# A norm split in two, gate derivatives from a table, stores on another queue, and 31 VectorE steps given to GpSimd

## The chip, the cores and the metric

The kernel runs on one core of a Trainium2 chip. Its time is the device time of one execution in microseconds (us), and the median of several runs is what counts. Engines are named as in the profile: PE (TensorE, matrix products; PEld is its weight load), DVE (VectorE), ACT (ScalarE), POOL (GpSimd), SP (SyncE, which here only issues DMAs).

## The reference

A sequence of 2048 positions with 512 channels is normalized; one branch is a short convolution of `k` times `v`, then a convolution over the whole sequence by FFT; the other is a gated MLP of width 1376. The kernel computes the output and the gradients of all nine inputs used.

```python
xn = _layernorm(A_q)
# branch s
k_shift = sum_t k_pad[:, t:t+S] * shift_k[:, ks-1-t]      # 4 taps
kv = k_shift * v
y  = irfft(rfft(kv, 2S) * rfft(ssm_k, 2S))[:S] + kv * ssm_D
s  = xn * y
# branch g
z  = (sigmoid(xn @ w_gate) * (xn @ w_up)) @ w_down
out = x + s * silu(z)
# returned: out, and the gradients for grad_out of A_q, A_k, A_v, A_shift_k, A_ssm_k, A_ssm_D, B_w_gate, B_w_up, B_w_down
```

## The kernel before

The sequence lies as 128 partitions by 16 rows (NJ). `p` counts 8 pairs of row tiles (256 positions), `cg` 4 groups of 128 channels, `q` two halves of an FFT block. Almost all of SBUF is one tile, `slab`, divided by hand, and PSUM is one tile, `psum`; so the profile names nearly everything `slab` and `psum`, and one line, L479, which calls every recorded operation.

The work falls into three stages that overlap.

- Front: `ln(p)` normalizes a pair of tiles (`bn_stats` and `bn_aggr` on DVE, the power −1/2 on GpSimd, the small product `nmr` on DVE, the scaling with its shift on DVE or ACT) and transposes the result; `gu_gen(p)` and `z_gen(p)` are the MLP; `strK`, `strV` and `strX` transform the long filter, build `kv` (four products over `lag`, 3 first, with sums between them) and go forward and back through the FFT. `step1`, `step2`, `inv2` and `inv1` are FFT steps as matrix products, each followed by an evacuation of PSUM (`evac`: on ACT or DVE, whichever queue holds it) and, for some, by a transpose on DVE.
- Middle: `zs_pre(p)` and `zs_gen(p)` form the gate silu(z), its derivative, `out_0` and `dz`; `dh_gen` and `x_gen` go back through the MLP. `zs_pre` runs two activations on ACT and three products and sums of 1024 columns on DVE for each pair.
- Back: `dW` makes the three weight gradients (`out_9`, `out_7`, `out_8`) with its operands loaded back transposed from DRAM (`hD`, `dgD`, `duD`), and stores each piece through one of three buffers `ot`; between its pieces `frontC` and `backC` carry the gradient of the convolution: products of 2048 columns with the kept spectra `KK` and `VV`, `inv2` and `inv1`, then `dks = dkv * v` and `dkv = dkv * ksh` for each `cg`, the four lags into `dk` (`out_2`), and `out_3` from `dkv`.

Nothing is scheduled while the kernel runs. All operations are first recorded with a number each; the table `ORDER` gives, for each of the five engines, the numbers in the order of its queue, and `BANKS` the PSUM bank of each tile. The `Rec.order` method checks that the queues can proceed and emits them. An engine works its queue strictly in order: an instruction that waits holds all behind it. DMAs stand in the queue of the engine that issues them, SP for nearly all.

Of the kernel before, what the change touches and what calls it, by code (L numbers as in the profile page):

```python
# [8 lines left out]
ACT = mybir.ActivationFunctionType  # L9
ALU = mybir.AluOpType  # L10
# [58 lines left out]
    """,  # L69
    "vector": """  # L70
# [1364 lines left out]
```

## Time and profile before

| | |
|---|---|
| runs | 469.19, 463.36, 464.43 us; median 464.43 |
| profiled execution, its own time | 466.05 us |
| its span, first to last instruction | 464.3 us |
| mean granted clock of TensorE | 0.987 |
| DMA | 117.13 MB in 188798 packets |

In the parts that follow, a group's line gives the engine, the operation, what is written from what (partitions x elements, type), the count, then busy us in all and the mean ns of one, then the idle time of the engine just before it and what ended it. A line of the timeline gives the start, the length, the engine, the operation and the count, and in brackets the wait ahead of it. A line of windows gives a stretch, its length, and the busy us of each engine with the number of instructions.

### The profile page before, as it was taken

What the parts mean: (1) busy time and instruction counts of PE and PEld (TensorE: products, weight loads), DVE (VectorE), ACT (ScalarE), POOL (GpSimd) and SP (SyncE); (2) the same over time, 40 slices, a digit from 0 to 9 for tenths busy, and PEclk for the clock granted to TensorE, in tenths of its full rate; (3) what the DMA queues carried; (4) which work ended last, traced back from release to release, by engine and by line L of the source; (5) the groups of instructions that cost most, each with busy time, mean ns of one, the idle gap of its engine ahead of it and who ended that gap; (6) DMA issues with size and microseconds to landing.
All of it is one profiled execution on the core that took longest, in us unless ns stands there. A gap on an engine that the chain in (4) does not pass through costs nothing.

```text
span 464.3 us, 11690 instructions
## 1 busy us (share of the span) xinstructions
PE 443.4 (95%) x4934; PEld 306.4 (66%) x4963; DVE 420.5 (91%) x634; ACT 287.8 (62%) x368; POOL 15.5 (3%) x31
## 2 busy tenths in 40 slices
PE   6998999999999999999999999999999799999994
PEld 3867785758667677556655664444467678877883
DVE  8999999999999899999999976679998799999991
ACT  7767898888667646565563433377744676855331
POOL 4200110010000000000000000000000000000000
PEclk8899899999999999999999999999999999999999
DMA  7999877869378799989689999799998999999997
GB/s 247 367 332 240 270 240 262 253 230 300 101 230 286 196 218 254 259 262 319 167 260 200 313 297 271 179 343 240 261 263 197 254 231 254 249 212 242 192 327 272
DMA packets 188798, 117.13 MB, mean 252 GB/s; under 512 B 107541, under 2 KB 175049, under 8 KB 188234
## 3 DMA queue, kind: packets, MB, share of 16 engines
q1 hardware_dynamic: 187546, 115.99, 92.3%
q8 instruction: 39, 0.64, 0.6%
q10 hardware_dynamic: 1200, 0.39, 0.4%
q14 instruction: 13, 0.11, 0.1%
HBM read 43.74 MB, written 46.70 MB: 195 GB/s over the span
## 4 chain that ended last, share of the span: by engine, by line
PE 60%; DVE 10%; DMA 6%; issue 2%; SPq 1%; ACT 1%; DVEq 0%; ACTq 0%
PE psum L479 60%; DVE slab L479 10%; DMA slab<-duD 3%; DMA slab<-KD 2%; SPq L479 1%; DMA slab<-VD 1%; ACT slab L479 1%; DMA out_dram<-slab 1%; DVEq L479 0%; ACTq L479 0%
## 5 line engine op out<-in xcount | busy, mean ns | idle before, releaser
L479 PE MATMUL psum<-slab 128*128 128x256 bf16 (+5 forms) x4934 | 443.4, 304 | 14.1 <-ACT slab L479 5.2
L479 PEld LDWEIGHTS <-slab 128*128 128x128 bf16 (+2 forms) x4963 | 306.4, 96 | 150.9 <-issue 39.0
L479 ACT CAST slab<-psum 128x1024 bf16<-128x1024 f32 (+4 forms) x233 | 202.4, 914 | 124.1 <-PE psum L479 71.3
L479 DVE TENSOR_TENSOR slab<-slab 128x1024 bf16<-128x1024 bf16 (+5 forms) x322 | 251.8, 821 | 21.5 <-ACT slab L479 13.3
L479 DVE STREAM_TRANSPOSE slab<-slab 128x1024 f32<-128x1024 f32 x48 | 76.2, 1591 | 2.4 <-ACT slab L479 1.6
L479 ACT ACTIVATE slab<-slab 128x512 bf16<-128x512 bf16 (+5 forms) x58 | 49.1, 880 | 26.3 <-DVE slab L479 24.5
L479 ACT ACTIVATE slab<-psum 128x512 bf16<-128x512 f32 (+1 forms) x56 | 32.3, 576 | 14.6 <-PE psum L479 13.3
L479 DVE CAST slab<-psum 128x1024 bf16<-128x1024 f32 (+2 forms) x32 | 34.2, 1073 | 6.4 <-PE psum L479 5.0
L479 DVE TENSOR_TENSOR slab<-psum,slab 128x512 bf16<-128x512 f32 (+2 forms) x52 | 31.2, 603 | 1.3 <-PE psum L479 1.1
L479 DVE SCALAR_TENSOR_TENSOR slab<-slab 128x2 f32<-128x2 f32 (+1 forms) x40 | 14.2, 366 | 1.5 <-POOL slab L479 1.2
L479 POOL MEMSET slab<- 128x128 bf16 (+3 forms) x10 | 5.2, 535 | 299.0 <-PE psum L479 153.0
L479 DVE TENSOR_SCALAR slab<-slab 128x512 bf16<-128x512 bf16 (+9 forms) x40 | 10.8, 285 | 0.2
L479 POOL TENSOR_TENSOR slab<-slab 128x2 f32<-128x2 f32 x8 | 8.3, 1039 | 74.5 <-DVE slab L479 74.5
L479 DVE BATCH_NORM_STATS2 slab<-slab 128x6 f32<-128x512 bf16 x16 | 10.5, 671 | 0.0
L479 ACT COPY slab<-psum 128x512 bf16<-128x512 bf16 (+1 forms) x9 | 6.7, 777 | 2.7 <-PE psum L479 2.6
L479 DVE SCALAR_TENSOR_TENSOR slab<-psum,slab 128x512 bf16<-128x512 f32 x8 | 5.5, 686 | 2.2 <-PE psum L479 2.1
L479 ACT ACT_TABLE_LOAD x4 | 5.1, 1283 | 2.3 <-issue 2.2
L479 DVE COPY slab<-psum 128x512 bf16<-128x512 bf16 (+1 forms) x9 | 4.8, 531 | 0.6 <-PE psum L479 0.6
L479 DVE MEMSET slab<- 32x192 uint32 (+3 forms) x10 | 1.4, 144 | 1.5 <-PE psum L479 1.1
L479 DVE BATCH_NORM_AGGREGATE slab<-slab 128x2 f32<-128x6 f32 x16 | 2.6, 165 | 0.0
L479 POOL IOTA slab<- 128x32 f32 (+3 forms) x8 | 2.0, 270 | 0.4 <-POOLq L1419 0.4
L479 ACT ACTIVATION_READ_ACCUMULATOR slab<-psum 128x1 f32 x8 | 1.6, 199 | 0.0
(10 smaller groups left out, 6.2 us busy)
## 6 DMA issues: line engine op xcount, KB each, us to landing
slab<-KD SPq DMA_DIRECT2D x16, 512.0 KB, 4.9
hD<-slab SPq DMA_DIRECT2D x8, 704.0 KB, 6.2
dgD<-slab SPq DMA_DIRECT2D x8, 704.0 KB, 7.0
duD<-slab SPq DMA_DIRECT2D x8, 704.0 KB, 4.8
slab<-in_A_k_dram SPq DMA_DIRECT2D x4, 1024.0 KB, 6.5
KD<-slab SPq DMA_DIRECT2D x8, 512.0 KB, 6.5
VD<-slab SPq DMA_DIRECT2D x8, 512.0 KB, 4.9
out_dram<-slab SPq DMA_DIRECT2D x16, 256.0 KB, 4.5
```

The lines of the kernel that those rows point to most:

```text
L479: getattr(getattr(self.nc, eng), meth)(*[place(v) for v in a], **{x: place(v) for x, v in k.items()})
```

## The change

1. The first norm (`p == 0`) is worked tile by tile: statistics and power of tile 0, then of tile 1, then the scalings. Its memset of the warm-up operand is on DVE, 13 warm-up matmuls stand for 10, and 5 more follow the transposes of the first two tiles. The tables for the FFT come after it in the recording, and the weights' first 256 columns before it.
2. The gate and its derivative come from ACT's tables `Silu` and `Derivative_silu`, two pairs at a time (`zs_batch`), for six of the eight pairs; the two pairs made inside `strG` keep `zs_pre`. ACT loads 11 tables for 4.
3. The weight gradients are evacuated on ACT alone and stored from ACT's queue, through 5 buffers `ot` for 3.
4. GpSimd gets the scaling of the norm for `p >= 2` (12), the product of lag 3 in `strV` (4), the sum `x + s` for `out_0` (8), `dkv * ksh` (4) and the product of lag 0 in `backC` but for the last group (3): 31 in all.
5. `ORDER` and `BANKS` are new throughout, and a sixth list, `moves`, gives the order of all DMAs over both issuing queues.

```diff
@@ ORDER
     "tensor": """
-        4+9 222 220 216 218 58+3 63+3 150+7 141+7 102+15 167+7 281 285+3 282+2 159+7 135+3 130+3 187+15 178 182+3
+        7+12 229 227 231 161+7 152+7 40 233 35+3 41+3 46+3 189+7 113+15 170+15 412+7 384+7 236+7 198+15 146+3 141+3
...
@@ Rec.order
-            for eng, q in queue.items():
+            for eng in self.ENGS:
+                q = queue[eng]
                 while at[eng] < len(q):
                     op = ops[q[at[eng]]]
+                    if moves and "dma" in op.alts[0][1] and moves[-1] != op.n:
+                        break
...
@@ ln
-        nc.vector.tensor_scalar_add(ve, sv[:, :, 7], LN_EPS)
-        nc.gpsimd.tensor_tensor(out=r, in0=ve, in1=neghalf.to_broadcast([P, 2]), op=ALU.pow)
-        nc.vector.scalar_tensor_tensor(nmr, sv[:, :, 6], -1.0, r, ALU.mult, ALU.mult)
-        for t in range(2):
-            u, m, b = x[:, t], r[:, t:t + 1], nmr[:, t:t + 1]
-            nc.add([("scalar", "activation", (u, u, ACT.Identity), dict(bias=b, scale=m))][p == 0:]
-                   + [("vector", "tensor_scalar", (u, u, m, b, ALU.mult, ALU.add), {})])
+        def stats(a, b):
...
+            nc.gpsimd.tensor_tensor(out=r[:, a:b], in0=ve[:, a:b], in1=neghalf.to_broadcast([P, b - a]), op=ALU.pow)
+        def norm(a, b):
+            nc.vector.scalar_tensor_tensor(nmr[:, a:b], sv[:, a:b, 6], -1.0, r[:, a:b], ALU.mult, ALU.mult)
+            for t in range(a, b):
+                u, m, c = x[:, t], r[:, t:t + 1], nmr[:, t:t + 1]
+                (nc.vector if p < 2 else nc.gpsimd).tensor_scalar(u, u, m, c, ALU.mult, ALU.add)
+        for a, b in ((0, 1), (1, 2)) if p == 0 else ((0, 2),):
+            stats(a, b)
+        for a, b in ((0, 1), (1, 2)) if p == 0 else ((0, 2),):
+            norm(a, b)
...
+                if p == 0:
+                    nc.vector.tensor_copy(dst, src)
+                    warm(x[:, t, 0:128], 3 * t + 1)
...
+    def zs_batch(ps_):
+        for p in ps_:
+            gate = T[p]["gate"] = wk["gate"].next()
+            nc.scalar.activation(gate, stA["zA"][:, 2 * p:2 * p + 2, :], ACT.Silu)
+        for p in ps_:
+            z = stA["zA"][:, 2 * p:2 * p + 2, :]
+            nc.scalar.activation(z, z, ACT.Derivative_silu)
...
-    nc.gpsimd.memset(warm_r.ap, 0.0)
+    nc.vector.memset(warm_r.ap, 0.0)
...
@@ strV
-                    nc.vector.tensor_tensor(acc, src, skl, ALU.mult)
+                    nc.gpsimd.tensor_tensor(out=acc, in0=src, in1=skl, op=ALU.mult)
@@ zs_gen
-        nc.vector.tensor_tensor(x, x, s, ALU.add)
+        nc.gpsimd.tensor_tensor(out=x, in0=x, in1=s, op=ALU.add)
@@ strZ
-            if "gate" not in T[p]:
-                zs_pre(p)
+            zs_next(n)
@@ dW
-                    nc.evac(ot[0:kf, :], acc[0:kf, :], 512)
-                    nc.sync.dma_start(out_9[f0 + b * 128:f0 + b * 128 + kf, :], ot[0:kf, :])
+                    nc.scalar.copy(ot[0:kf, :], acc[0:kf, :])
+                    nc.scalar.dma_start(out_9[f0 + b * 128:f0 + b * 128 + kf, :], ot[0:kf, :])
...
-                nc.evac(ot[:, :, 0:w], acc[:, :, 0:w], 2 * w)
+                nc.scalar.copy(ot[:, :, 0:w], acc[:, :, 0:w])
...
@@ backC
-            nc.vector.tensor_tensor(dkv, dkv, ksh, ALU.mult)
+            nc.gpsimd.tensor_tensor(out=dkv, in0=dkv, in1=ksh, op=ALU.mult)
...
-                    if lag == 0:
+                    if lag == 0 and cg < NG - 1:
+                        nc.gpsimd.tensor_tensor(out=dk, in0=src, in1=skl, op=ALU.mult)
+                    elif lag == 0:
                         nc.vector.tensor_tensor(dk, src, skl, ALU.mult)
```

What this does to the queues is seen at three places. GpSimd in the front, before: the 128x2 products are the powers of the norms, `1x768` the zeros ahead of a load of `k`.

```order
L479 TENSOR_TENSOR slab<-slab 128x2
L479 IOTA slab 128x32
L479 MEMSET slab 32x512
L479 TENSOR_TENSOR slab<-slab 128x2 x3
L479 MEMSET slab 1x768
L479 TENSOR_TENSOR slab<-slab 128x2 x2
L479 MEMSET slab 128x4x32
```

The same place after: 128x512 is the scaling of one tile, 128x2048 the product of lag 3.

```order
L492 TENSOR_TENSOR slab<-slab 128x2 x3
L492 TENSOR_SCALAR slab<-slab 128x512
L492 TENSOR_TENSOR slab<-slab 128x2
L492 TENSOR_SCALAR slab<-slab 128x512 x3
L492 TENSOR_TENSOR slab<-slab 128x2048
L492 TENSOR_SCALAR slab<-slab 128x512
L492 TENSOR_TENSOR slab<-slab 128x2
L492 TENSOR_SCALAR slab<-slab 128x512
L492 TENSOR_TENSOR slab<-slab 128x2
L492 TENSOR_TENSOR slab<-slab 128x2048
```

The powers, for which DVE waits, now stand behind scalings and products.

SP in the last third of the back, before: transposed loads (`duD`) and loads of kept tensors with the stores of `out_8` (128x2x256) between them.

```order
L479 DMA out_dram<-slab 128x2x256
L479 DMA slab<-VD_68 128x2048
L479 DMA slab<-slab 15x384
L479 DMA_TRANSPOSE slab<-duD_98 128x8x256 x2
L479 DMA out_dram<-slab 128x2x256 x2
L479 DMA slab<-kshD_60 128x2048
L479 DMA_TRANSPOSE slab<-duD_97 128x8x256
L479 DMA out_dram<-slab 128x2x256
L479 DMA_TRANSPOSE slab<-duD_98 128x8x256
```

ACT near its end, after: each store now follows evacuations (CAST from `psum`) on the same queue.

```order
L492 CAST slab<-psum 128x8x128
L492 DMA out_dram<-slab 128x2x256
L492 CAST slab<-psum 128x512
L492 DMA out_dram<-slab 128x2x256 x2
L492 CAST slab<-psum 128x512
L492 DMA out_dram<-slab 128x2x256
L492 CAST slab<-psum 128x128x8
```

SP keeps the loads and the stores of the other outputs; 35 stores moved over.

DVE near the end of the back, before: the first 128x16x128 sum belongs to the third channel group, the second is `dkv * ksh` of the last one, and 128x8x128 and 128x1024 are halves of the last group's lags.

```order
L479 TENSOR_TENSOR slab<-slab 128x2048
L479 TENSOR_REDUCE slab<-slab 128x4
L479 TENSOR_TENSOR slab<-slab 128x16x128
L479 TENSOR_TENSOR slab<-slab 128x1024
L479 TENSOR_TENSOR slab<-slab 128x8x128
L479 TENSOR_TENSOR slab<-slab 128x16x128
L479 TENSOR_TENSOR slab<-psum,slab 128x128
```

The same place after:

```order
L492 TENSOR_TENSOR slab<-slab 128x16x128
L492 TENSOR_TENSOR slab<-slab 128x2048 x2
L492 TENSOR_REDUCE slab<-slab 128x4
L492 MEMSET slab 32x192
L492 TENSOR_TENSOR slab<-slab 128x8x128
L492 TENSOR_TENSOR slab<-slab 128x16x128
L492 CAST slab<-psum 128x128x8
L492 COPY slab<-slab 128x1
```

The product with `ksh` is gone to GpSimd's queue, and an evacuation (128x128x8) that ACT had has come in its place.

More of the change, by code (lines that the diff above doesn't have):

```diff
@@ L33 @@
     "tensor": """
[35 rows of a table removed]
[29 rows of a table added]
     """,
     "vector": """
[26 rows of a table removed]
[23 rows of a table added]
     """,
     "scalar": """
[15 rows of a table removed]
[17 rows of a table added]
     """,
     "gpsimd": """
-        20 68 19 3 31+1 69 98 41 53 71+1 70 210 99 125 73 100 472 1628 883 906 1900 1297 2232 3538 4769
+        52 109 81 53 79+1 20 110 21 25 84 83 29 111 82 73 136 221 483 224 894 896 223 485 235 897 1911 486 1308 579
+        1914 1639 917 1913 1310+1 1078 1538 1642 1641 2278 2243 2419 2722 2855 2992 3123 3256 3383 3531 3921 4277 4762
+        4528 4681 5241 5398 5838
     """,
     "sync": """
[12 rows of a table removed]
[11 rows of a table added]
+    """,
+    "moves": """
[12 rows of a table added]
     """,
@@ L133 @@
 BANKS = (
-    "11312331001230100111001001100111000011100101101010101010110010110001110001010011011021013001101001100001110120"
-    "11000101100110011100011000110100110201301111010021112030101013323110130103201032101131010310122111230102312112"
-    "20012110031202212022032102122210023212013202301211212022210100203221102123221220123101210220300120131122203320"
-    "2202213202203023223032"
+    "02030110310012300101110310011302110011100101010101101201103010101110000011011031001010201031100101100111000001"
+    "21301110100110011002311001110010110010101100001011000211010101001130101010020011011013010003010311011001030011"
+    "20020210013210121202310220200201010232122122113021220102203202121030210221230022201221001021312002121303201220"
+    "213203212013101102002112"
 )
@@ L456, in order @@
                         owner[b] = v
-        seq, at = [], {e: 0 for e in queue}
+        seq, at, moves = [], {e: 0 for e in self.ENGS}, queue["moves"][::-1]
         while len(seq) < len(ops):
             had = len(seq)
-            for eng, q in queue.items():
+            for eng in self.ENGS:
+                q = queue[eng]
                 while at[eng] < len(q):
                     op = ops[q[at[eng]]]
+                    if moves and "dma" in op.alts[0][1] and moves[-1] != op.n:
+                        break
                     if not all(ops[d].done for d in op.deps) or any(w.left for v in op.tiles for w in before[id(v)]):
@@ L466, in order @@
                     op.done = True
+                    if moves and moves[-1] == op.n:
+                        moves.pop()
                     for v in op.tiles:
@@ L470, in order @@
             if len(seq) == had:
-                raise RuntimeError("the order is stuck at " + str({e: q[at[e]:at[e] + 1] for e, q in queue.items()}))
+                raise RuntimeError("the order is stuck at " + str({e: queue[e][at[e]:at[e] + 1] for e in self.ENGS}))
         return seq
@@ L685, in ln @@
         x, st = xnA[:, 2 * p:2 * p + 2, :], lnst.next()
-        for t in range(2):
-            nc.vector.bn_stats(st[:, 8 * t:8 * t + 6], x[:, t])
-        for t in range(2):
-            nc.vector.bn_aggr(st[:, 8 * t + 6:8 * t + 8], st[:, 8 * t:8 * t + 6])
         sv = st[:, 0:16].rearrange("p (t x) -> p t x", x=8)
@@ L692, in ln @@
         r = rstd_all[:, 2 * p:2 * p + 2]
-        nc.vector.tensor_scalar_add(ve, sv[:, :, 7], LN_EPS)
-        nc.gpsimd.tensor_tensor(out=r, in0=ve, in1=neghalf.to_broadcast([P, 2]), op=ALU.pow)
-        nc.vector.scalar_tensor_tensor(nmr, sv[:, :, 6], -1.0, r, ALU.mult, ALU.mult)
-        for t in range(2):
-            u, m, b = x[:, t], r[:, t:t + 1], nmr[:, t:t + 1]
-            nc.add([("scalar", "activation", (u, u, ACT.Identity), dict(bias=b, scale=m))][p == 0:]
-                   + [("vector", "tensor_scalar", (u, u, m, b, ALU.mult, ALU.add), {})])
+        def stats(a, b):
+            for t in range(a, b):
+                nc.vector.bn_stats(st[:, 8 * t:8 * t + 6], x[:, t])
+            for t in range(a, b):
+                nc.vector.bn_aggr(st[:, 8 * t + 6:8 * t + 8], st[:, 8 * t:8 * t + 6])
+            nc.vector.tensor_scalar_add(ve[:, a:b], sv[:, a:b, 7], LN_EPS)
+            nc.gpsimd.tensor_tensor(out=r[:, a:b], in0=ve[:, a:b], in1=neghalf.to_broadcast([P, b - a]), op=ALU.pow)
+        def norm(a, b):
+            nc.vector.scalar_tensor_tensor(nmr[:, a:b], sv[:, a:b, 6], -1.0, r[:, a:b], ALU.mult, ALU.mult)
+            for t in range(a, b):
+                u, m, c = x[:, t], r[:, t:t + 1], nmr[:, t:t + 1]
[4 more added lines that the diff above has]
+            norm(a, b)
         if p + 2 < NP:
@@ L707, in ln @@
                     nc.tensor.transpose(pt[:, db, :], x[:, t, db * 128:(db + 1) * 128], ident)
-                nc.evac(xnT[:, t].rearrange("p d k -> p (d k)"), pt[:].rearrange("p a k -> p (a k)"), 512)
+                dst, src = xnT[:, t].rearrange("p d k -> p (d k)"), pt[:].rearrange("p a k -> p (a k)")
+                if p == 0:
+                    nc.vector.tensor_copy(dst, src)
+                    warm(x[:, t, 0:128], 3 * t + 1)
+                else:
+                    nc.evac(dst, src, 512)
         else:
@@ L768, in zs_pre, with zs_next @@
         nc.vector.tensor_tensor(z, tm, sg, ALU.add)
+    def zs_batch(ps_):
[5 more added lines that the diff above has]
+            nc.scalar.activation(z, z, ACT.Derivative_silu)
+    def zs_next(n):
+        if "gate" not in T[ORD[n]]:
+            if n == 2:
+                wk["gate"].extend(wk["sg"])
+                wk["gate"].extend(wk["tm"])
+            zs_batch(ORD[n:n + 2])
     def ld_KT(cg, eng=None):
@@ L792, in ld_w, with warm @@
             e.dma_start(w[:, :, f0:f1], src[:, f0:f1].rearrange("(db p) f -> p db f", p=P))
+    def warm(w, n):
+        pw = ps("w", [512])
+        for _ in range(n):
+            nc.tensor.matmul(pw[:], w, warm_r.ap[:, 0:512], start=True, stop=True)
     f_ld(0)
+    ld_w(0, 256, nc.sync, nc.scalar)
     ld_KT(0)
     warm_r = Ring(ar, [640])
-    nc.gpsimd.memset(warm_r.ap, 0.0)
-    pw = ps("w", [512])
-    for _ in range(10):
-        nc.tensor.matmul(pw[:], warm_r.ap[:, 512:640], warm_r.ap[:, 0:512], start=True, stop=True)
-    ld_w(0, 256, nc.sync, nc.scalar)
+    nc.vector.memset(warm_r.ap, 0.0)
+    nc.vector.memset(neghalf, -0.5)
+    warm(warm_r.ap[:, 512:640], 13)
+    make_identity(nc, ident)
+    f_ln(0)
+    tabs = gen_fft_tables(nc, ar, negpi, halfpi, Cf)
     nc.scalar.dma_start(Dcol_b, A_ssm_D.rearrange("(cg p) -> p cg", p=P))
-    tabs = gen_fft_tables(nc, ar, negpi, halfpi, Cf)
-    make_identity(nc, ident)
+    f_ld(1)
     ld_w(256, 768, nc.sync, nc.sync)
     nc.sync.dma_start(skr, A_shift_k.rearrange("(o d) t -> o (d t)", o=1))
-    f_ld(1)
     ld_w(768, F, nc.sync, nc.sync)
@@ L811, in kernel_impl @@
     ld_v()
-    nc.vector.memset(neghalf, -0.5)
     nc.vector.memset(ones1, 1.0)
-    f_ln(0)
     gen_fft_consts(nc, ar, negpi, TT, I32, tabs)
@@ L1149, in strZ @@
             flags.add(("z", n))
-            if n + 1 < NP and "gate" not in T[ORD[n + 1]] and ("zf", ORD[n + 1]) in flags:
-                zs_pre(ORD[n + 1])
+            if n + 1 < NP and ("zf", ORD[n + 1]) in flags:
+                zs_next(n + 1)
     def strD():
@@ L1181, in kernel_impl @@
                        until=lambda: ("dh", 7) in flags)
-    for r in [WdT_r, x2_r, dzT_r, sig_r, h_r] + list(wk.values()):
+    for r in [WdT_r, x2_r, dzT_r, sig_r, h_r] + [wk[k] for k in ("s", "a", "gg", "gate")]:
         r.free()
@@ L1187, in kernel_impl @@
             (Ring, [NJ, GW], 1), (Ring, [512], 1), (Ring, [256], 1), (Ring, [GW], 1))
-    L_r, Xc_r, QV_r, QtV_r, ot_r = ar.rings((Ring, [NJ, 256], 3), (Ring, [2, 2048], 2), (WRing, 2048, 1), (WRing, 1024, 1), (Ring, [512], 3),
+    L_r, Xc_r, QV_r, QtV_r, ot_r = ar.rings((Ring, [NJ, 256], 3), (Ring, [2, 2048], 2), (WRing, 2048, 1), (WRing, 1024, 1), (Ring, [512], 5),
                                             freed=[b for r in dead for b in r.blks], then=late)
@@ L1229, in dW @@
                     ot = ot_r.next().rearrange("p (b f) -> p b f", b=2)
-                    nc.evac(ot[:, :, 0:w], acc[:, :, 0:w], 2 * w)
-                    nc.sync.dma_start(out[d2 * 256:(d2 + 1) * 256, f0:f0 + w].rearrange("(b p) f -> p b f", p=P), ot[:, :, 0:w])
+                    nc.scalar.copy(ot[:, :, 0:w], acc[:, :, 0:w])
+                    nc.scalar.dma_start(out[d2 * 256:(d2 + 1) * 256, f0:f0 + w].rearrange("(b p) f -> p b f", p=P), ot[:, :, 0:w])
             if n == 5:
```

178 rows, old and new, of the table ORDER are left out of this document.

## The prediction

> **What bounds the kernel now.** I read the page first, for the share of each engine.
>
> ```profile
> span 464.3 us, 11690 instructions
> PE 443.4 (95%) x4934; PEld 306.4 (66%) x4963; DVE 420.5 (91%) x634; ACT 287.8 (62%) x368; POOL 15.5 (3%) x31
> ...
> DVE  8999999999999899999999976679998799999991
> ...
> POOL 4200110010000000000000000000000000000000
> ...
> PE psum L479 60%; DVE slab L479 10%; DMA slab<-duD 3%; DMA slab<-KD 2%; SPq L479 1%; DMA slab<-VD 1%; ACT slab L479 1%; DMA out_dram<-slab 1%; DVEq L479 0%; ACTq L479 0%
> ```
>
> TensorE and VectorE are both nearly full, GpSimd is empty. TensorE holds 60% of the last chain, VectorE 10%. A share of the whole span hides stages, so the windows come next: front (12 to 156), middle (156 to 300), back (300 to 456).
>
> ```profile
> 0.00:12.00 12.00, 7.94 (x41) 4.53 (x42) 10.56 (x39) 9.10 (x10) 5.30 (x18) 0.84 0.80 251
> 12.00:36.00 24.00, 23.95 (x243) 18.48 (x243) 22.96 (x53) 17.14 (x24) 3.01 (x7) 0.94 0.99 344
> 36.00:48.00 12.00, 10.53 (x127) 8.54 (x125) 11.96 (x22) 10.33 (x13) 0.84 (x1) 0.90 1.18 265
> 48.00:60.00 12.00, 11.95 (x113) 8.80 (x113) 11.38 (x18) 10.36 (x14) 1.93 (x3) 0.95 0.72 208
> 60.00:84.00 24.00, 22.42 (x284) 15.45 (x283) 23.42 (x27) 20.58 (x26) 1.19 (x1) 1.00 0.84 270
> 84.00:156.00 72.00, 71.49 (x915) 50.43 (x920) 71.16 (x76) 54.01 (x72) 1.80 (x2) 1.00 0.71 231
> 156.00:300.00 144.00, 143.26 (x937) 89.09 (x950) 127.77 (x259) 73.28 (x103) 0.73 (x1) 1.00 0.97 250
> 300.00:360.00 60.00, 58.74 (x782) 33.59 (x788) 53.90 (x54) 38.10 (x45) 0.00 (x0) 1.00 1.00 253
> 360.00:372.00 12.00, 9.53 (x142) 7.65 (x141) 8.86 (x8) 7.65 (x9) 0.00 (x0) 1.00 1.10 259
> 372.00:456.00 84.00, 82.06 (x1338) 68.51 (x1337) 78.14 (x84) 46.05 (x56) 0.73 (x1) 1.00 1.04 247
> 456.00:465.00 9.00, 1.50 (x33) 1.36 (x32) 0.36 (x1) 1.21 (x3) 0.00 (x0) 0.84 0.58 219
> ```
>
> After the length stand the busy times of PE, PEld, DVE, ACT and POOL, then the clock granted to TensorE. In the front PE is busy 140.3 of 144 us (3.7 idle) and DVE 140.9 (3.1 idle): both bind. In the middle PE is full (0.7 idle) and DVE has 16.2 us to spare. In the back PE has 5.7 us idle of 156, DVE 140.9 busy and 15.1 idle. So a faster VectorE can win at most the 9.4 us of PE idle in front and back, plus something at the two ends; a slower VectorE costs soon in the front and later in the back.
>
> **The change, part by part.** First what is taken from DVE, and the one thing that can be said of GpSimd's prices.
>
> ```profile
> L479 DVE TENSOR_TENSOR slab<-slab 128x2048 bf16<-128x2048 bf16 x109 | 129.9, 1211 | 7.1 <-DMA slab<-KD 3.1 <-ACT slab L479 2.1 <-DMA slab<-VD 1.0
> L479 DVE TENSOR_TENSOR slab<-slab 128x1024 bf16<-128x1024 bf16 x150 | 97.3, 684 | 4.9 <-ACT slab L479 3.2 <-DVE slab L479 0.8
> ...
> L479 DVE CAST slab<-psum 128x1024 bf16<-128x1024 f32 x25 | 30.1, 1209 | 1.1 <-PE psum L479 0.8
> ...
> L479 POOL TENSOR_TENSOR slab<-slab 128x2 f32<-128x2 f32 x8 | 8.3, 1039 | 74.5 <-DVE slab L479 74.5
> ...
> L479 DVE TENSOR_SCALAR slab<-slab 128x512 bf16<-128x512 bf16 x13 | 5.6, 440 | 0.0
> ...
> L479 ACT ACT_TABLE_LOAD x4 | 5.1, 1283 | 2.3 <-issue 2.2
> ...
> L479 POOL MEMSET slab<- 1x768 bf16 x4 | 2.9, 727 | 248.0 <-DVE slab L479 146.0 <-PE psum L479 102.0
> ...
> L479 POOL MEMSET slab<- 128x640 bf16 x1 | 0.6, 631 | 0.0
> ```
>
> DVE loses 11 products of 2048 columns (4 in the convolution of the front, 7 in the back), 13.3 us; 26 steps of 1024 columns (18 of the gate derivatives, 8 sums of out_0), 17.8 us; 9 scalings, 4.0 us. The new order gives it 8 more evacuations of 1024 columns, 9.7 us. Net it is some 25 us lighter.
>
> GpSimd takes 11 products, 8 sums and 12 scalings (3 of these from ScalarE). No trace shows it on such tiles. Its memsets of 640 and 768 columns differ by 96 ns, 0.75 ns a column. A product reads two operands and writes one: between one and three times that rate, plus up to the 0.69 us of its smallest product (quoted next), gives 1.5 to 5.3 us for 2048 columns. I take 3.5, between the ends, since no row is nearer to either; 1.8 for 1024 and 1 for a scaling: about 65 us in all, which fits into an idle engine.
>
> The price lies elsewhere: do the two engines run side by side? The timeline of DVE and POOL, at two places:
>
> ```profile
> 46.99 1.22 DVE L479 TENSOR_TENSOR slab<-slab 128x2048 bf16<-128x2048 bf16 x1
> 47.16 1.59 POOL L479 TENSOR_TENSOR slab<-slab 128x2 f32<-128x2 f32 x1 [12.88 <-DVE slab L479]
> ...
> 48.78 0.16 DVE L479 SCALAR_TENSOR_TENSOR slab<-slab 128x2 f32<-128x2 f32 x1 [0.58 <-POOL slab L479]
> ```
> ```profile
> 12.54 0.69 POOL L479 TENSOR_TENSOR slab<-slab 128x2 f32<-128x2 f32 x1 [0.24 <-DVE slab L479]
> ...
> 13.34 0.74 DVE L479 TENSOR_SCALAR slab<-slab 128x512 bf16<-128x512 bf16 x1
> 13.41 0.52 POOL L479 MEMSET slab<- 32x512 bf16 x1
> ```
>
> The same two-column power takes 0.69 us at 12.54 and 1.59 at 47.16, where it starts inside a DVE product and ends 0.54 us after it (48.75 against 48.21): GpSimd was held until the product was over. The other way round, a DVE scaling beside a GpSimd memset takes 0.74 us against a mean of 0.44 and ends 0.15 us after the memset: VectorE was held. So I count a DVE product that comes up while a GpSimd product runs as held to its end. The Trainium skill has this as a rule (SBUF — State Buffer, "Who interferes with whom"): a DVE instruction with two SBUF inputs contends with a GpSimd instruction that reads SBUF, and whoever starts first keeps the shared ports for its whole instruction. The rows agree, except that none shows a DVE product held. GPSIMD Engine Reference, section 3.1, measures 4497 ns for a 2048-column fp32 tensor_tensor on GpSimd; with that price in place of my 3.5 us the sum below would come to about 476.
>
> How much of each is held follows from how often DVE meets such a product; its groups in the front, then in the back:
>
> ```profile
> L479 DVE TENSOR_TENSOR slab<-slab 128x2048 bf16<-128x2048 bf16 x48 | 57.5, 1209 | 0.5 <-ACT slab L479 0.2
> ```
> ```profile
> L479 DVE TENSOR_TENSOR slab<-slab 128x2048 bf16<-128x2048 bf16 x61 | 72.3, 1213 | 6.7 <-DMA slab<-KD 3.1 <-ACT slab L479 1.9 <-DMA slab<-VD 1.0
> ...
> L479 DVE TENSOR_TENSOR slab<-slab 128x1024 bf16<-128x1024 bf16 x14 | 9.4, 686 | 0.9 <-DVE slab L479 0.8
> ...
> L479 DVE TENSOR_TENSOR slab<-slab 128x512 bf16<-128x512 bf16 x5 | 2.0, 400 | 0.0
> ```
>
> *Start.* Today PE waits 1.83 us for the first norm; below, the row, and the weight load that now stands ahead of the second input tile on ScalarE's queue.
>
> ```profile
> 8.46 1.04 PE L479 MATMUL psum<-slab 128*128 128x128 bf16 x8 [1.83 <-DVE slab L479]
> ```
> ```profile
> 1.64 0.53 ACTq L479 DMA_DIRECT2D slab<-in_B_w_up_dram  x1
> ```
>
> The norm of one tile no longer waits for the other; the second tile's issue moves back by 0.53 us behind the weights. Taken −1 us; bounds −2.5 (wait and some cold clock gone) and +0.5 (the late tile decides).
>
> *Front.* Other DVE work between two products averages (140.9 − 57.5) / 48 = 1.7 us, so a 3.5 us product holds DVE for 1.8: four of them, 7.2. Twelve scalings are shorter than that gap: 0.3 each, 3.6. Less 4.8 + 4.0 freed, that is +2 on DVE, which has 3.1 idle. Taken +1. Also the power now stands in GpSimd's queue behind products; behind it DVE's scaling waits (0.58 us above), and with that all evacuations queued there: up to 4.5 us once, in the upper bound. Bounds −4 (not held, PE's idle gone) to +8.
>
> *Middle.* 17.8 us off DVE count nothing: PE is full. ScalarE takes 7 table loads, 9.0 us, into 70.7 us of its own idle time; if an evacuation is due just then, PE waits up to 1.3 us each. The 8 sums write out_0 only; the buffer they free is due a stage later. Taken 0; bounds −0.5 to +4.
>
> *Back.* Two-input products are 83.7 of 140.9 us, in 80 pieces: 0.7 us between two, so a 3.5 us product holds DVE for 2.8. Seven: 19.6; less 8.5 freed, plus about 3 of the added evacuations: +14 on DVE against 15.1 idle, of which the KD and VD loads keep part. I let 9 be absorbed: +5. Bounds −5 (not held) to +15.
>
> *Stores.* Weight-gradient stores go from SyncE's queue to ScalarE's, with 5 output buffers for 3.
>
> ```profile
> ACT slab L479 <- DMA out_dram<-slab: 20.7, 7, 5.1
> ```
> ```profile
> 448.89 2.91 ACT L479 CAST slab<-psum 128x1024 bf16<-128x1024 f32 x4 [5.11 <-DMA out_dram<-slab]
> ```
> ```profile
> 450.44 1.74 PE L479 MATMUL psum<-slab 128*128 128x96 bf16 x34 [0.46 <-ACT slab L479]
> ```
>
> ScalarE stands 20.7 us for buffers, but PE feels 0.46 us of it here, and loads behind SyncE's stores some more. 35 issues at about 0.5 us fit ScalarE's 64 us of idle time in the back. What is late next is the last matmul and its store, which stay. Taken −2; bounds 0 to −4.
>
> Sum: 464.3 − 1 + 1 + 0 + 5 − 2 = 467.3. The profiled execution took 466.05, 1.75 outside its span, and the median shown is 464.43, 1.6 lower; both together add 0.1. **467 us.**
>
> **Rivals.**
>
> *The lock decides (slower).* Place: the back. If a product on GpSimd takes over 4 us, DVE's 15 us of idle time are used up and each further microsecond goes to PE. At 4.4 us, halfway from my value to the upper end: back 7 × 3.7 + 3 − 8.5 − 9 = +11, front 4 × 2.7 + 3.6 − 8.8 − 3 = +3: 464.3 − 1 + 3 + 11 − 2 = 475. At 5.3, the end: back +18, front +6, 485. For it: both directions of holding are in the trace. Against it: the holding pow reads two columns only, and a product may let go between pieces. Chance 0.30, 474 to 488.
>
> *GpSimd runs free (faster).* A product on it doesn't hold DVE. Then the 9.4 us of PE idle in front and back go, or most of it: 464.3 − 1.5 − 3 − 4 − 2 = 454. For it: the cover of 25 us on DVE is real. Against it: the 1.59 us row. Chance 0.18, 450 to 460.
>
> *Nothing moves.* PE is its own bound, DVE's idle absorbs every hold, and the stores' waits were hidden: 463. Chance 0.10.
>
> **How the numbers follow.** My forecast, 460 to 474 around 467, has 0.42. A measurement of this kernel tells about 2% from no change: 455.1 and 473.7. Faster: most of the free case, 0.15. Slower: nearly all of the lock case and the upper end of the forecast, 0.33. Same: 0.52. The range runs from 454 to 482; about a tenth lies beyond either end. The forecast's own is 460 to 474.
>
> **What would show it.** Right: GpSimd products of 3 to 4 us; DVE products of 2048 columns with a tail of 2 us and more over 1.21 at those places; DVE's busy time in the back not below today's 140.9; ScalarE's wait for out_dram gone; PE's first transposes earlier by a microsecond. Wrong: products on DVE still at 1.21 us while GpSimd works (then the free case), GpSimd products over 4.4 us (then the lock case), or a power behind a product for which DVE waits more than 3 us at several places.

## The result, and the profile after

The changed kernel takes 489.28 us (median of 4 runs, 488.47 to 490.78) against 464.83 for the kernel before in the same session: ratio 1.0502, 95% interval 1.0452 to 1.0553. The ratio is taken over the fast runs of both kernels, so it differs a little from the quotient of the medians, 1.0526. The change is slower by 5%, outside the range forecast. The profiled execution took 488.47 us, its span 486.7.

The page of the changed kernel first: span, busy times, and the rows of DVE and POOL in 40 slices.

```profile
span 486.7 us, 11716 instructions
PE 448.9 (92%) x4938; PEld 307.4 (63%) x4971; DVE 434.1 (89%) x595; ACT 289.0 (59%) x368; POOL 93.8 (19%) x62
...
DVE  7889899999998788898988897899996998989993
...
POOL 4227342133000022120111010000024430025020
...
PE psum L492 10%; DVE slab L492 5%; DMA out_dram<-slab 2%; ACTq L492 0%; ACT slab L492 0%; DVEq L492 0%
```

GpSimd works 78.3 us more, as the diff says. But VectorE, with 39 instructions fewer, is busy 13.6 us *longer*. The chain at the end of the page covers only the last fifth of this span, so its 10% for PE can't be set against the 60% of before. The groups say which of DVE's instructions grew (count, then busy us in all and mean ns of one):

```profile
L492 DVE TENSOR_TENSOR slab<-slab 128x2048 bf16<-128x2048 bf16 x98 | 135.0, 1396 | 3.0 <-DMA slab<-KD 1.1 <-ACT slab L492 0.7 <-DMA slab<-in_A_k_dram 0.2
L492 DVE TENSOR_TENSOR slab<-slab 128x1024 bf16<-128x1024 bf16 x124 | 89.5, 752 | 7.5 <-ACT slab L492 5.1 <-DMA slab<-hD 0.9 <-PE psum L492 0.5
...
L492 DVE CAST slab<-psum 128x1024 bf16<-128x1024 f32 x33 | 40.0, 1215 | 5.7 <-PE psum L492 5.0 <-ACT slab L492 0.4
...
L492 POOL TENSOR_TENSOR slab<-slab 128x2048 bf16<-128x2048 bf16 x11 | 49.4, 4499 | 169.6 <-DMA slab<-kshD 66.9 <-DVE slab L492 58.3 <-ACT slab L492 18.2
L492 POOL TENSOR_TENSOR slab<-slab 128x1024 bf16<-128x1024 bf16 x8 | 18.8, 2346 | 149.9 <-DVE slab L492 114.1 <-DMA slab<-in_A_q_dram 29.7 <-PE psum L492 6.1
L492 POOL TENSOR_SCALAR slab<-slab 128x512 bf16<-128x512 bf16 x12 | 13.2, 1104 | 1.3 <-DVE slab L492 1.3
```

The mean of a DVE product with both operands in `slab` went from 1211 to 1396 ns at 2048 columns, from 684 to 752 at 1024; an evacuation from PSUM stayed (1209, now 1215). So DVE as a whole did not become slower. The timeline shows where the added time sits, at three places (start, length, engine, operation):

```profile
105.72 6.18 DVE L492 TENSOR_TENSOR slab<-slab 128x2048 bf16<-128x2048 bf16 x2
...
105.71 5.11 POOL L492 TENSOR_TENSOR slab<-slab 128x2048 bf16<-128x2048 bf16 x1 [18.19 <-ACT slab L492]
...
111.96 0.41 PE L492 MATMUL psum<-slab 32*32 32x512 bf16 x8 [3.49 <-DVE slab L492]
...
362.22 1.97 DVE L492 STREAM_TRANSPOSE slab<-slab 128x1024 f32<-128x1024 f32 x1
364.22 1.23 DVE L492 CAST slab<-psum 128x1024 bf16<-128x1024 f32 x1
...
361.87 4.06 POOL L492 TENSOR_TENSOR slab<-slab 128x2048 bf16<-128x2048 bf16 x1 [66.89 <-DMA slab<-kshD]
...
385.24 10.05 DVE L492 TENSOR_TENSOR slab<-slab 128x2048 bf16<-128x2048 bf16 x2
...
385.02 8.05 POOL L492 TENSOR_TENSOR slab<-slab 128x2048 bf16<-128x2048 bf16 x2
...
395.34 0.62 PE L492 MATMUL psum<-slab 32*32 32x512 bf16 x8 [5.29 <-DVE slab L492]
```

At 105.7 two DVE products, 2.4 us of work, take 6.18, and PE stands 3.49 us for what follows them. At 361.9 a GpSimd product runs beside a DVE transpose and a DVE evacuation, and neither is lengthened. At 385.0 GpSimd has two products back to back, and two DVE products end only at 395.29, 2.2 us after the second; PE has then stood 5.29 us. Summed over the trace (each DVE instruction's length over the usual one of its shape, where it overlaps a GpSimd instruction; stream transposes left out, which have two usual lengths, 1.2 and 2.0 us), DVE was held 35.6 us: 10.7 beside the 4 products of the front, 10.1 beside the 8 sums, 14.4 beside the 7 products of the back, 0.6 beside the 12 scalings. How that reaches TensorE is in the waits (us in total, times, longest), of the kernel before first:

```profile
PE psum L479 <- DVE slab L479: 3.6, 3, 1.8
```
```profile
PE psum L492 <- DVE slab L492: 23.2, 20, 5.3
...
ACT slab L492 <- DMA out_dram<-slab: 6.9, 3, 3.1
```

PE waited 3.6 us for DVE before, now 23.2. ScalarE's wait for store buffers fell from 20.7 to 6.9, as the change intended. The windows place it (length; busy PE, PEld, DVE, ACT, POOL; granted clock):

```profile
84.00:156.00 72.00, 63.79 (x803) 44.69 (x814) 68.23 (x60) 52.88 (x66) 11.11 (x4) 0.95 0.59 188
156.00:300.00 144.00, 137.54 (x1009) 86.82 (x1022) 128.63 (x229) 84.38 (x113) 19.65 (x10) 1.00 0.94 250
...
372.00:456.00 84.00, 75.02 (x1191) 60.53 (x1190) 79.27 (x63) 42.74 (x53) 20.30 (x6) 0.96 1.02 226
```

PE lost 7.7 us of busy time in the front's window (71.49 before), 5.7 in the middle, which had been full (143.26), and 7.0 in the back (82.06). In either trace some 30 matmul records are missing (29 and 33, against the weight loads), so each of these is good to about a microsecond.

Waiting is not all of it. The clock of the first and the last of these windows was 1.00 before and is 0.95 and 0.96 now. The drops lie at three long waits of PE, of 2.79, 3.49 and 5.29 us, which end at 89.3, 112.0 and 395.3:

```profile
89.50:92.90 3.40, 3.40 (x27) 2.90 (x25) 3.40 (x5) 1.93 (x2) 0.00 (x0) 0.50 0.24 86
113.40:116.80 3.40, 3.40 (x32) 1.88 (x30) 3.27 (x5) 2.49 (x4) 0.00 (x0) 0.50 0.61 182
393.30:400.10 6.80, 4.25 (x39) 2.38 (x39) 6.71 (x7) 2.84 (x3) 0.00 (x0) 0.50 1.12 287
```

What that is worth is seen below, where two kernels with the same matmuls are compared. That the waits cause the drops is not shown: in a later run (the fills below) the clock also fell to 0.50 from 125.5 on, with no wait of PE over 1.3 us before it in the whole front.

### The profile page after: what moved, and what is told of

Same layout as the page of the kernel before. It is cut to its first block, busy times and chain, and to the rows that moved or that the text cites. A ratio compares the mean times of both kernels' runs of the same rounds, so it can differ in the third digit from the quotient of the medians.

```text
span 486.7 us, 11716 instructions
## 1 busy us (share of the span) xinstructions
PE 448.9 (92%) x4938; PEld 307.4 (63%) x4971; DVE 434.1 (89%) x595; ACT 289.0 (59%) x368; POOL 93.8 (19%) x62
## 5 line engine op out<-in xcount | busy, mean ns | idle before, releaser
L492 PE MATMUL psum<-slab 128*128 128x256 bf16 (+5 forms) x4938 | 448.9, 306 | 31.9 <-DVE slab L492 23.2
L492 ACT CAST slab<-psum 128x1024 bf16<-128x1024 f32 (+4 forms) x229 | 197.1, 902 | 161.5 <-PE psum L492 104.3
L492 DVE TENSOR_TENSOR slab<-slab 128x1024 bf16<-128x1024 bf16 (+4 forms) x285 | 255.8, 932 | 14.8 <-ACT slab L492 7.1
L492 POOL TENSOR_TENSOR slab<-slab 128x2048 bf16<-128x2048 bf16 (+3 forms) x28 | 74.3, 2657 | 341.0 <-DVE slab L492 193.9
L492 ACT ACTIVATE slab<-slab 128x512 bf16<-128x512 bf16 (+5 forms) x55 | 47.0, 886 | 16.9 <-DVE slab L492 16.7
L492 DVE CAST slab<-psum 128x1024 bf16<-128x1024 f32 (+2 forms) x36 | 42.0, 1170 | 8.7 <-PE psum L492 8.0
L492 DVE SCALAR_TENSOR_TENSOR slab<-slab 128x2 f32<-128x2 f32 (+2 forms) x41 | 17.9, 440 | 3.7 <-ACT slab L492 3.4
L492 POOL TENSOR_SCALAR slab<-slab 128x512 bf16<-128x512 bf16 x12 | 13.2, 1104 | 1.3 <-DVE slab L492 1.3
L492 DVE BATCH_NORM_STATS2 slab<-slab 128x6 f32<-128x512 bf16 x16 | 10.7, 679 | 0.0
L492 POOL MEMSET slab<- 128x128 bf16 (+2 forms) x9 | 4.2, 471 | 28.6 <-DVE slab L492 17.9
L492 DVE TENSOR_SCALAR slab<-slab 128x2 f32<-128x2 f32 (+9 forms) x32 | 6.6, 232 | 0.1
```

Of the source, the lines that this page charges most:

```text
L492: getattr(getattr(self.nc, eng), meth)(*[place(v) for v in a], **{x: place(v) for x, v in k.items()})
```

## The experiments

**Theory.** A DVE instruction with two operands in SBUF is held while a GpSimd instruction reads SBUF, and these holds are the 5%. **Rivals.** The new order, the split norm or the stores cost it; or GpSimd's results come late and their consumers wait.

**All 31 steps back.** Everything else of the change stays: first norm, gate tables, stores, order of the other engines.

```diff
-                    nc.gpsimd.tensor_tensor(out=acc, in0=src, in1=skl, op=ALU.mult)
+                    nc.vector.tensor_tensor(out=acc, in0=src, in1=skl, op=ALU.mult)
...
-        nc.gpsimd.tensor_tensor(out=x, in0=x, in1=s, op=ALU.add)
+        nc.vector.tensor_tensor(out=x, in0=x, in1=s, op=ALU.add)
...
-            nc.gpsimd.tensor_tensor(out=dkv, in0=dkv, in1=ksh, op=ALU.mult)
+            nc.vector.tensor_tensor(out=dkv, in0=dkv, in1=ksh, op=ALU.mult)
...
-                        nc.gpsimd.tensor_tensor(out=dk, in0=src, in1=skl, op=ALU.mult)
+                        nc.vector.tensor_tensor(out=dk, in0=src, in1=skl, op=ALU.mult)
```

(and the same for the scalings in `ln`; in `ORDER` their numbers go from the list `gpsimd` into `vector`).

> The changed kernel with all 31 steps back on VectorE, each put into VectorE's queue where GpSimd had begun it in the trace of the changed kernel; everything else (first norm, gate tables, stores, order of the other steps) stays. Lock theory (a product on VectorE is held while GpSimd reads SBUF; 35.6 us of held time in the trace): the held time goes and about 25 us of work return to VectorE, so PE's extra idle time of 23 us goes almost wholly: 462, between 457 and 468. Rival (the new order, the gate tables or the stores cost the time): still above 480.

Measured: 469.62 us (10 runs), ratio 1.0021, interval 0.9983 to 1.0059. Of its page and its waits:

```profile
PE 448.2 (96%) x4971; PEld 306.5 (65%) x4971; DVE 419.3 (89%) x626; ACT 288.7 (62%) x368; POOL 14.7 (3%) x31
```
```profile
PE psum L492 <- DVE slab L492: 9.8, 15, 1.3
```

DVE does 31 steps more than in the changed kernel and is busy 14.8 us *less*; the longest wait of PE for DVE falls from 5.3 to 1.3 us. So the 31 steps carry the loss, and what is left of the change is worth nothing that can be measured here. It is not the gain expected, 462 us with 468 as the upper end: that part of the expectation missed.

**One kind of step at a time.** The same edit for the 11 products alone, the 8 sums alone and the 12 scalings alone.

> Only the 11 products of 2048 columns go back to VectorE; 8 sums and 12 scalings stay on GpSimd. Lock theory: 25.0 us of the 35.6 us held go, and with them the gaps of PE at 86, 108 and 390 us (2.95, 3.66 and 5.64 us); left are the stalls of the middle, some 6 us: 470, between 465 and 475. Rival (order): above 480.

> Only the 8 sums of 1024 columns go back to VectorE. Lock theory: 10.1 us of held time go, and the PE stalls of about 0.75 to 1.3 us beside each sum in the middle: 489 less 5 to 7, so 483. Prediction's own term for the middle (0, PE is full there): 489, no change.

> Only the 12 scalings of the norms go back to VectorE. Lock theory: they held VectorE for 0.6 us in all, so nothing comes back, and 12 x 0.4 us of work goes to VectorE in the stage where it is nearly full: 489 to 494. If GpSimd's scalings cost by the powers queued behind them: below 486.

Measured: products back 473.69 us, ratio 1.0132 (1.0094 to 1.0170); sums back 484.79, 1.0365 (1.0334 to 1.0397); scalings back 491.50, 1.0492 (1.0434 to 1.0551). Against the changed kernel's 1.0502, from the session before, the products are worth 3.7 points, the sums 1.4, and the scalings 0.1, which is inside the intervals of about 0.6 either way: no cost of a scaling on GpSimd is shown, and no gain. PE's busy time and its waits for DVE, of the kernel with the products back, and then of that with the sums back:

```profile
PE 448.2 (95%) x4971; PEld 306.3 (65%) x4971; DVE 422.9 (90%) x606; ACT 288.3 (61%) x368; POOL 47.7 (10%) x51
...
PE psum L492 <- DVE slab L492: 11.0, 15, 1.3
```
```profile
PE 452.2 (94%) x4971; PEld 308.6 (64%) x4971; DVE 428.4 (89%) x603; ACT 288.8 (60%) x368; POOL 75.6 (16%) x54
...
PE psum L492 <- DVE slab L492: 21.0, 13, 5.8
```

The products make the long waits, of up to 5 us and more. The sums make a few short ones in the middle: with them on GpSimd PE stands idle 4.5 us there (between the marks used further below), in waits of up to 1.2 us; with all 31 steps back it is 0.6. And where the products stay on GpSimd, the same 4971 matmuls take 4.0 us longer (452.2 for 448.2), at a mean granted clock of 0.977 for 0.991: that much of their cost is not waiting.

**Is it the reading?** GpSimd is kept as busy, but with fills in place of products and sums.

```diff
+def BESIDE(nc, out, in0, in1, op):
+    n = out.shape[1]
+    nc.gpsimd.tensor_tensor(out=out[:, 0:1, 0:1], in0=in0[:, 0:1, 0:1], in1=in1[:, 0:1, 0:1], op=op)
+    nc.gpsimd.memset(out, 0.0)
+    nc.gpsimd.memset(out[:, n // 4:n], 0.0)
...
+                if op.n in GIVEN:
+                    BESIDE(self.nc, **k)
+                    continue
```

> The changed kernel, with each of the 11 products and 8 sums that GpSimd got replaced on GpSimd by a tensor_tensor of one element (it keeps the wait for both inputs) and two fills of the same output region, of 2048 and 1536 columns (1024 and 512 for a sum). So GpSimd is occupied about as long (some 3.5 us for a product by the 0.95 us per 1000 columns of the 768-column fill), but reads almost no SBUF while it is; the products and sums are not computed (the outputs are zeros there). Theory (DVE instructions with two SBUF inputs are held while a GpSimd instruction reads SBUF): no held DVE products are left beside these, the time falls to that of the kernel with all 31 steps back, 469.6, or up to 4 us below it, since DVE does not do those steps: 466 (462 to 472). Rival 1 (the results come late from a slow engine, and their consumers wait): as long as the changed kernel, 485 to 490. Rival 2 (writes of GpSimd hold DVE too): 480 to 490, with held products beside the fills.

Measured: 464.25 us (10 runs), ratio 0.9933 (0.9896 to 0.9971). The groups of DVE and POOL:

```profile
L496 DVE TENSOR_TENSOR slab<-slab 128x2048 bf16<-128x2048 bf16 x98 | 117.5, 1217 | 3.2 <-DMA slab<-KD 1.3 <-ACT slab L496 0.8
L496 DVE TENSOR_TENSOR slab<-slab 128x1024 bf16<-128x1024 bf16 x124 | 81.2, 685 | 10.0 <-ACT slab L496 7.0 <-DMA slab<-hD 1.5 <-PE psum L496 0.5
...
L505 POOL MEMSET slab<- 128x2048 bf16 x11 | 19.9, 1807 | 3.8 <-ACT slab L496 3.2
L506 POOL MEMSET slab<- 128x1536 bf16 x11 | 15.2, 1378 | 0.6
```

And its timeline at the front's last product:

```profile
100.44 2.32 DVE L496 TENSOR_TENSOR slab<-slab 128x2048 bf16<-128x2048 bf16 x2
...
100.00 1.80 POOL L505 MEMSET slab<- 128x2048 bf16 x1
101.86 1.38 POOL L506 MEMSET slab<- 128x1536 bf16 x1
```

The same 98 and 124 DVE products are back at 1217 and 685 ns; two of them take 2.32 us beside the fills where they took 6.18 beside a product. GpSimd is busy 3.52 us for each product's place (0.34 for the one element, 1.81, 1.38), a little less than a product's 4.06, so lateness is cut too, by about half a microsecond; but a fill that held DVE's products would have shown in the means. Nor did the zeros that the fills leave raise the granted clock (0.985 in the profiled execution, 0.991 with all 31 back). What holds DVE's two-operand products is the reading. The Trainium skill says just this (SBUF — State Buffer, "Who interferes with whom"): two SBUF inputs on DVE contend with a GpSimd instruction that reads SBUF, not with one that only writes. Both halves agree with these runs. But a fill is not free for all of DVE: once, at 34.45, a TENSOR_SCALAR of 128x128, which has one tensor operand, took 1.92 us beside a fill, and in the other kernels it takes 0.21 to 0.23.

This kernel leaves out work, so it is no candidate; it shows about the most that these 31 steps could bring in this order if GpSimd did not hold DVE: 0.7% against the kernel before.

**Shorter pieces.**

```diff
+def BESIDE(nc, out, in0, in1, op):
+    w = 512 // out.shape[2]
+    for c in range(0, out.shape[1], w):
+        nc.gpsimd.tensor_tensor(out=out[:, c:c + w], in0=in0[:, c:c + w], in1=in1[:, c:c + w], op=op)
```

> The changed kernel, with each GpSimd product and sum issued as pieces of 512 columns, back to back (4 for a product, 2 for a sum). Theory A (the hold ends with the GpSimd instruction, and the waiting DVE product goes next): a DVE product is held for one piece, at most 1.3 us, in place of 2 to 5 us; of 35.6 us of holds some 15 stay, and the time is 475 to 482. Theory B (DVE is not let in between GpSimd instructions that follow at once, as beside the two products at 385 us): the hold lasts as long as before or longer by the fixed cost of three more instructions: 489 to 495, with single DVE products of 5 us and more beside the pieces.

Measured: 481.19 us, ratio 1.0286 (1.0211 to 1.0361); holds of 27.4 us in all for 35.6. Two places of its timeline:

```profile
102.45 3.62 DVE L496 TENSOR_TENSOR slab<-slab 128x2048 bf16<-128x2048 bf16 x2
...
100.62 6.46 POOL L505 TENSOR_TENSOR slab<-slab 128x512 bf16<-128x512 bf16 x4 [12.11 <-ACT slab L496]
...
379.60 10.91 DVE L496 TENSOR_TENSOR slab<-slab 128x2048 bf16<-128x2048 bf16 x2
...
379.37 8.91 POOL L505 TENSOR_TENSOR slab<-slab 128x512 bf16<-128x512 bf16 x8
```

At 102 the engines take turns: DVE is let in between two pieces, and GpSimd pays with 6.46 us for four pieces. At 379 they do not: GpSimd runs eight pieces in 8.91 us and the first of the two DVE products takes 9.77 of the 10.91. Theory A holds in the front and gains two points; at this one place B holds. What sets the two apart is not settled. Nor do turns help everywhere: the sums, now two pieces each, still held DVE 9.6 us for 10.1, and the table below has the gain in the front alone.

**Two steps left.** The 8 sums and 9 products go back; GpSimd keeps the scalings and the first group's `dkv` and `dk` product, beside which DVE transposed and evacuated.

```diff
-            nc.gpsimd.tensor_tensor(out=dkv, in0=dkv, in1=ksh, op=ALU.mult)
+            (nc.gpsimd if cg == 0 else nc.vector).tensor_tensor(out=dkv, in0=dkv, in1=ksh, op=ALU.mult)
```

> The changed kernel with the 8 sums and 9 of the 11 products back on DVE, at the places of the kernel with all 31 back; GpSimd keeps the 12 scalings and the two back products (the first group's dkv and dk) beside which DVE ran no held instruction. Theory (only steps that meet two-input DVE instructions cost): DVE is 8 us shorter there and nothing is held: 468 (465 to 471), the same as the kernel before or a little below that with all 31 back (469.6). Rival (any GpSimd product in the back costs, since its result is later): 472 to 475.

Measured: 468.85 us (10 runs), ratio 1.0044 (1.0008 to 1.0081); the two products take 4.06 us each and hold no DVE instruction. As the theory has it, they cost nothing that can be measured; but what they free is not felt either. No version that computes everything beat the kernel before.

## Why the prediction was wrong

All versions of the changed order pass the same marks, so the loss can be split by stage: the front ends at the start of DVE's 24th stream transpose of 48, the middle at the 25th. Of one profiled execution each (us, worked out from the timeline's starts and the span; executions of one kernel spread by some 3 us either way):

| kernel | front | middle | back |
|---|---|---|---|
| changed | 165.9 | 128.2 | 192.6 |
| all 31 back | 157.5 | 123.3 | 187.9 |
| products back | 156.1 | 127.9 | 188.0 |
| sums back | 167.3 | 122.8 | 192.5 |
| fills in their place | 157.1 | 121.8 | 184.2 |
| pieces of 512 | 159.1 | 129.0 | 191.6 |

Against all 31 back the steps cost 8.4 us in the front, 4.9 in the middle and 4.7 in the back, 18 in all, where the prediction's terms had 1, 0 and 5.

- **What bounds the kernel** was read rightly: a slower VectorE did cost in the front. That DVE "has 16.2 us to spare" in the middle did not protect that stage.
- **The price of a GpSimd product** was taken as 3.5 us. It is 4.06 alone and 4.93 to 5.13 when it first waits for a DVE product to end, 4.50 on the mean; 2.35 for a sum (taken 1.8), 1.10 for a scaling (taken 1). The Trainium skill's 4497 ns (GPSIMD Engine Reference, section 3.1) was nearer than my mid-value; on bf16 the product alone is a tenth below it.
- **Front, +1: the step that failed.** Not the holds: they were put at 7.2 + 3.6 = 10.8 us and measured 10.7 + 0.6. What failed is setting freed time against them, "Less 4.8 + 4.0 freed, that is +2 on DVE, which has 3.1 idle". DVE's own sum came out much as forecast: it is busy 151.5 us up to the mark and 148.4 with all 31 back, +3 for the +2. Yet the stage grew by 8.4. The kernel with fills frees the same DVE time and holds nothing, and reaches the mark at 157.1; the kernel with all 31 back frees nothing and reaches it at 157.5. The holds cost 8.8 (165.9 − 157.1), over the upper bound of +8, and the freed time brought 0.4. That last figure is less sure: PE stood idle 5.7 us in the front with fills and 8.4 with all back, but at a mean clock of 0.97 against 0.99, so up to some 3 us of a gain may be hidden in it. The changed kernel's PE stood idle about 15 us. A hold stops DVE's queue for 2 to 4 us at one place, with the transposes and evacuations that PE needs behind it, and time freed elsewhere did not give that back. The drop of the clock at the longest waits has no term in the sum at all.
- **Middle, 0: failed too.** I asked who waits for the sums' results ("write out_0 only") and not whom they hold. The eight held DVE for 10.1 us, and the stage is 6.4 us longer than with fills and 5.4 longer than with the sums back; the upper bound was +4.
- **Back, +5:** about right as a number, and by luck. Against all steps back it is 4.7 longer, against products back 4.6. But the holds are 14.4 us where I counted 19.6, two of seven products falling beside transposes and evacuations, which are not held; with 14.4 my own sum, less 8.5 freed and 9 absorbed, plus 3, comes to about 0. Here too the netting was wrong: against fills the back is 8.4 longer.
- **Start −1 and Stores −2:** the store waits went as said (20.7 to 6.9 us), yet the kernel with all 31 back, which keeps both, is at 1.0021 and not at the 0.9936 of −3. The start explains part: it came later, not earlier. The first scaling, before and then after, and what stood ahead of it in DVE's queue:

```profile
7.81 0.96 DVE L479 TENSOR_SCALAR slab<-slab 128x512 bf16<-128x512 bf16 x3
```
```profile
8.20 0.16 DVE L492 TENSOR_TENSOR slab<-slab 128x1 bf16<-128x1 bf16 x1 [2.28 <-DMA slab<-in_A_ssm_D_dram]
...
9.75 0.40 DVE L492 TENSOR_SCALAR slab<-slab 128x512 bf16<-128x512 bf16 x1
```

DVE stood 2.28 us for the load of `in_A_ssm_D` between the first norm's statistics and its scaling (1.48 with all 31 back). DVE's first product that reads PSUM, for the MLP, starts at 17.54, with all 31 back at 16.58, and before at 15.47: about 1 us lost without the 31 steps, not 1 won. Where the other 2 us or so of these terms went was not tried.
- **The rival that the lock decides** was the right one, and its condition, a product over 4 us, came true. It gave 474 to 488, a little below the 489 measured, and by its own sum a product of 4.5 us makes only 476: it too set freed time against held. It placed most of the loss in the back; the runs put front 8.8, middle 6.4, back 8.4 above the kernel with fills, 23.6 in all, which is the difference of the spans (486.7 − 463.2 = 23.5). It missed the middle altogether.
- **The rows for the lock:** the power held inside a DVE product was the right one to go by. The scaling of 0.74 us beside a fill is of another kind, with one tensor operand and beside a GpSimd instruction that only writes, and says nothing on products.

## What to carry to other kernels

Before giving elementwise work to GpSimd, list what VectorE runs at that moment: here a VectorE product with both operands in SBUF stood still until the GpSimd product beside it ended, while a transpose or an evacuation from PSUM ran on, and a fill on GpSimd did not hold the product. Don't set held time against freed time over a stage: of 35.6 us of holds 23.5 came out in the span (486.7 against 463.2 with fills), while of 18.8 us taken off VectorE (419.3 busy with all 31 back, 400.5 with fills) 5.5 did (468.7 against 463.2; one execution each). Ask of a moved step not only who needs its result but also whom it keeps from working.

## What was not expected of the hardware

- The hold goes both ways and adds up: a GpSimd product that starts inside a DVE product takes about 1 us longer (4.06 to 5.13), and then holds the next one.
- Instructions that follow at once on GpSimd can keep DVE out across their borders: one DVE product took 9.77 us beside eight pieces, while at other places DVE was let in after a piece.
- At three waits of TensorE, of 2.8 to 5.3 us, its granted clock was 0.50 for 3.4 to 6.8 us around or behind the end of the wait, so a hold may be paid twice; whether the one brings the other was not tested.
- GpSimd reads two operands at 1.98 ns a column (4.06 us for 2048) and fills at 0.88 (1.81 us); the 0.75 ns a column that I worked out from its small fills was near to the fill, and a product costs 2.2 times as much as the measured fill; I had allowed up to three times.
